# A table of block priorities, new durations in the build-time scheduler, and the first rope on VectorE

## The chip, the core and the metric

The kernel runs on one core of one Trainium2 chip. The engines of the core work side by side, each through its own list of instructions in order: TensorE (PE, matmuls, and PEld, the weight loads beside them), VectorE (DVE), ScalarE (ACT), GpSimd (POOL) and SyncE (SP), which here issues nearly all DMAs. An instruction that needs the work of another engine waits on a semaphore, and everything behind it on its engine waits too. The metric is the time of one execution on the device in microseconds (us), as a median of several runs.

## The reference

Attention over q, k and v with rotary embedding ("rope"), and then a gated MLP over the tokens of all heads together:

```python
batch, n_heads, seq, head_dim = (4, 8, 576, 64)
q_rot, k_rot = (rotate(q), rotate(k))
scores = scale * np.matmul(q_rot, k_rot.transpose(0, 1, 3, 2))
scores = scores - np.max(scores, axis=-1, keepdims=True)
attn = np.exp(scores)
attn = attn / (np.sum(attn, axis=-1, keepdims=True) + 1e-09)
out = np.matmul(attn, v)                       # then (B*S, H*D) = (2304, 512)
...
h = x @ w_in                                   # 512 x 2048
sp = np.where(h > 20.0, h, np.log1p(np.exp(np.minimum(h, 20.0))))
g = h * np.tanh(sp)                            # "mish"
return (g @ w_out).astype(np.float32)          # 2048 x 512
```

## The kernel before

The heads are taken in 16 pairs P (four pairs to a batch), the 576 queries of a pair in five steps t (four of 128 queries for each of the two heads, one of 64). I write (P,t) for a step. A step is: scores on PE into two PSUM pairs (line 569 or 563), the row maximum on DVE (577), exp on ACT (579), the reciprocal of the sums on DVE (588, 590). In the first batch (pairs 0 to 3, "exact" steps) PE itself transposes the weights (612, 625, 629), and ACT or DVE copies them to SBUF. In the other batches the weights are split into a high half (POOL 594 or ACT 596) and a low half (DVE 600), and a DMA transpose on SP turns them (678, and 689 for the step of 64). `av(P, k)` multiplies them with v (702 to 715) for the first 256 queries (k = 0, steps 0 and 1) and for the other 320 (k = 1), and ACT (736) and DVE (738) write the result as a high and a low half into `xt`.

Before a step comes the rope of its pair: `rope_turn` loads raw q or k by DMA (459, 462; a ring of three buffers), multiplies by cos and sin (469) and adds (473), in two column halves. All of it ran on POOL. From pair 8 on, ACT and POOL or DVE split the result once more (498 to 520). The weights w_in and w_out arrive as 64-bit numbers and are decoded block by block (829 to 849) on ACT, DVE and POOL during the first batch. v is loaded into a ring of two staging buffers (536, `stg`), scaled on ACT (539, 540), and POOL writes its low half (541) and so frees the buffer.

The MLP goes in eight chunks c (two for a batch, 256 and 320 tokens). `h_unit` does 12 matmuls (935) and mish on ACT (940), `h_split` makes the halves of g (950 or 951, 954), `p_sub` does 12 matmuls on g (971), four of which make an output block that ACT copies (979) and sends out. Exp and mish are in two ACT tables; each change of table is an instruction of its own (ACT_TABLE_LOAD).

All of this is recorded with `op(...)` as a list of operations with their possible engines, a duration in ns for each, and what they read and write. `Plan.order` then plays the list through at build time: it keeps a clock for each engine, and whenever one is free it gives it the ready operation with the lowest `prio` (the place in the list plus a shift, less a share of the longest chain behind it). What comes out is the order of the instructions of each engine, SP's DMAs among them. Where the plan has PE idle ahead of a matmul that takes a new PSUM buffer, `fill` puts matmuls on the identity there (1072), whose result nobody uses, to keep TensorE's clock up.

Of the kernel before, what the change touches and what calls it, by code (L numbers as in the profile page):

```python
# [39 lines left out]
TR = 107 / 128  # L40
ALPHA = 7
SLOTS = [
# [20 lines left out]
SWITCH = 1400  # L63
DWELL = 0
PEN = 202
PENP = 1
HOLD = 0
PE, ACT, DVE, POOL, SP = "PE", "ACT", "DVE", "POOL", "SP"


# [14 lines left out]
class Plan:  # L85
# [4 lines left out]
    def __init__(self):  # L90
        self.ops, self.rings, self.shift, self.banks = [], {}, 0, []

    def tile(self, pool, shape, dt, tag, bufs=1):
# [13 lines left out]
    def op(self, ways, w=(), r=(), table=None, after=()):  # L107
# [5 lines left out]
        o = {"ways": ways, "deps": set(), "users": [], "n": len(self.ops), "bufs": []}  # L113
        o["prio"] = o["n"] + self.shift
        if table:
# [25 lines left out]
    def order(self):  # L141
# [25 lines left out]
        ready_at = [0.0] * len(ops)  # L167
        free = dict.fromkeys((PE, ACT, DVE, POOL, SP), 0.0)
        ring_free = dma_free = 0.0
# [31 lines left out]
        while len(issued) < len(ops):  # L201
# [5 lines left out]
            for e in (PE, ACT, POOL, DVE, SP):  # L207
# [3 lines left out]
                while ready[e] or other:  # L211
# [58 lines left out]
                    else:  # L270
# [8 lines left out]
                        if e == PE:  # L279
                            if ops[n]["takes"] and 8000 < now < WARM:  # L280
                                b = ops[n]["takes"][0]
                                ends = [until(x) for x in held]
                                one = sum(ends[i] <= now for i in kinds[1])
                                at = min(ends[i] for i in kinds[2 if b.size == 2 or one <= b.keep else 1])
                                idle = 0.8 * (now - max(free[PE], at))
                                if idle > 350:
                                    while now - idle >= window + 3413:
                                        warm = busy > 2900 or (warm and busy > 1540)
                                        busy, window = max(busy - 3413, 0), window + 3413
                                    m = ops[n]["fill"] = int(idle / (108 if warm else 215))  # L290
                                    busy += m * (108 if warm else 215)
# [56 lines left out]
def pool_ns(n):  # L348
    return 2.39 * n + 20
# [15 lines left out]
def attention_mish_mlp(ctx: ExitStack, tc: tile.TileContext, qk, v, vflat, rope, ident_in, w_in, w_out, outT):  # L365
# [56 lines left out]
    def max_exponent(am, cols, lo, hi, out=None):  # L422
# [4 lines left out]
        pt = bank()  # L427
        op((PE, 110, lambda: nc.tensor.transpose(pt()[0:1, 0:128], m(), ident())), w=[pt], r=[m, ident])
        t = small((1, 1))
# [3 lines left out]
        pb = bank()  # L433
        op((PE, 60, lambda: nc.tensor.matmul(
            pb()[:, 0:1], e().to_broadcast([1, 128]), ident()[0:1, 0:1], start=True, stop=True)), w=[pb], r=[e, ident])
# [18 lines left out]
    def rope_turn(P, j, out=None, late=0):  # L454
# [9 lines left out]
        for c, s in enumerate(halves):  # L464
# [13 lines left out]
            op([(POOL, pool_ns(m), lambda f=add: f(nc.gpsimd), 1), (DVE, dve_ns(m), lambda f=add: f(nc.vector), 1)][:n],  # L478
               w=[(t, c) if out is None else (out, (j, c))], r=[(t, c), (t, 2 + c)])
# [104 lines left out]
    def inverse(sm, n, scale=2.0 ** -15):  # L584
        r = sbuf((128, 2), F32, "rs", 3)
        for h in range(n):
            c = slice(h, h + 1)
            op((DVE, 70, lambda c=c: nc.vector.tensor_scalar(sm()[:, c], sm()[:, c], 1e-9, scale, op0=ALU.add, op1=ALU.mult)),  # L588
               w=[(sm, h)])
            op((DVE, 80, lambda c=c: nc.vector.reciprocal(r()[:, c], sm()[:, c])), w=[(r, h)], r=[(sm, h)])  # L590
        return r
# [392 lines left out]
    def mlp(c):  # L984
        for u in range(8):
            for _ in h_unit(c, u):
                yield "h"
            if u >= 1:
                h_split(c, u - 1)
        h_split(c, 7)  # L990
        for e in range(4):
            for s in range(4):
                p_sub(c, e, s)
                yield "p"
# [15 lines left out]
    END = len(seq) + AVL + 1  # L1010

    def att(i):
        for f, a in aux.pop(i, []):
            f(*a)
        if i < len(seq):
            step(*seq[i])
        for f, a in aux.pop(("av", i), []):
            f(*a)

# [117 lines left out]
```

## Time and profile before

| what | value |
|---|---|
| time, median of 3 runs | 648.72 us (647.25 to 649.4) |
| profiled execution, span from the first to the last instruction | 652.7 us |
| PE busy | 615.1 us, 94% |
| ACT, DVE, POOL busy | 466.5, 414.9 and 270.9 us |
| mean granted TensorE clock | 0.991 |
| DMAs of SP | 60 transposes, 30 loads of raw q and k, 12 of v, and others |

The page gives the profiled execution's span alone as its own time; it lies 4.0 us over the median of the runs without a profile. A PE that is busy is not a PE that does needed work: the identity matmuls of `fill` count as busy. Idle time of an engine is put down to the instruction that ended it.

### The profile page before, as it was taken

The numbers are of one execution on the slowest core, as the hardware profiler recorded it, in microseconds if no ns is written. First come the engines' busy times: TensorE is split into PE (matmuls) and PEld (weight loads), VectorE is DVE, ScalarE is ACT, GpSimd is POOL, SyncE is SP. The second block draws the span as 40 slices with busy tenths as digits, with TensorE's granted clock in tenths as the row PEclk, the third lists the DMA queues.
The fourth block names the chain that finished last, engine by engine and source line by source line (L and its number), as shares of the span: only waits on it lengthen the run. The fifth ranks groups of instructions, "written<-read, shape, count | busy, mean of one in ns | idle before, by whom it ended". The sixth has DMA issues, their size and how long they took to land.

```text
span 652.7 us, 13278 instructions
## 1 busy us (share of the span) xinstructions
PE 615.1 (94%) x5218; PEld 458.3 (70%) x5218; DVE 414.9 (64%) x955; ACT 466.5 (71%) x856; POOL 270.9 (42%) x267
## 2 busy tenths in 40 slices
PE   3988889999998999899999999899999999999997
PEld 2665566777775656578877776588877777888775
DVE  0799999787586877747567777576567876211210
ACT  1679979999678995569979885597769956522520
POOL 5489878776937143433454355242212110000000
PEclk9998999999999999999999999899999999999999
DMA  8975415355396668755557664834344578000000
GB/s 321 422 277 173 165 65 170 105 186 159 122 199 123 146 127 189 128 118 93 118 119 160 110 156 100 167 62 74 71 89 91 76 146 137 13 9 17 9 12 31
DMA packets 143583, 82.52 MB, mean 126 GB/s; under 512 B 128160, under 2 KB 133920, under 8 KB 141984
## 3 DMA queue, kind: packets, MB, share of 16 engines
q1 hardware_dynamic: 138912, 76.95, 48.9%
q10 hardware_dynamic: 4608, 4.72, 2.2%
q8 instruction: 41, 0.67, 0.4%
q14 instruction: 22, 0.18, 0.1%
HBM read 45.09 MB, written 4.72 MB: 76 GB/s over the span
## 4 chain that ended last, share of the span: by engine, by line
PE 54%; DMA 2%; POOL 1%; issue 1%; ACT 1%; DVE 1%; DVEq 0%; POOLq 0%; ACTq 0%
PE bank L971 21%; PE bank L935 21%; PE pair L569 5%; PE bank L714 4%; DMA et<-ew 2%; PE pair L935 1%; PE pair L563 1%; PE bank L710 1%; DMA stg<-in_v 1%; POOL v L541 0%; POOL raw L473 0%; ACT e L579 0%; DVE mx L577 0%; POOL ew L594 0%; PE bank L715 0%
## 5 line engine op out<-in xcount | busy, mean ns | idle before, releaser
L971 PE MATMUL bank<-g,w 128*128 128x256 f16 (+1 forms) x1536 | 200.2, 287 | 0.9 <-DVE g L954 0.9
L935 PE MATMUL bank<-xt,w 128*128 128x320 f16 (+1 forms) x1440 | 187.0, 286 | 0.0
L971 PEld LDWEIGHTS <-w 128*128 128x128 f16 x1536 | 147.1, 98 | 47.6 <-issue 11.0
L935 PEld LDWEIGHTS <-w 128*128 128x128 f16 x1536 | 147.5, 98 | 42.9 <-issue 6.7
L579 ACT ACTIVATE e<-pair,mx 128x576 f32<-128x576 f32 x144 | 105.3, 735 | 37.1 <-DVE mx L577 32.7
L577 DVE TENSOR_REDUCE mx<-pair 128x1 f32<-128x576 f32 x144 | 103.4, 750 | 42.1 <-PE pair L569 38.2
L594 POOL TENSOR_SCALAR ew<-e,rs 128x576 f16<-128x576 f32 x68 | 51.3, 760 | 184.6 <-ACT e L579 94.4
L469 POOL TENSOR_TENSOR raw<-raw,cs 128x576 f32<-128x576 f32 (+2 forms) x64 | 90.1, 1425 | 42.7 <-DMA raw<-in_qk 42.2
L600 DVE SCALAR_TENSOR_TENSOR ew<-e,rs,ew 128x576 f16<-128x576 f32 x108 | 98.6, 949 | 13.3 <-ACT ew L596 7.3
L954 DVE SCALAR_TENSOR_TENSOR g<-mh,cells,g 128x512 f16<-128x512 f32 (+1 forms) x64 | 54.8, 865 | 65.5 <-ACT g L950 65.3
L569 PE MATMUL pair<-qk 64*128 64x288 f32 (+1 forms) x704 | 85.5, 362 | 3.5 <-ACT e L579 3.4
L940 ACT ACTIVATE mh<-bank,cells 128x256 f32<-128x256 f32 (+1 forms) x120 | 56.9, 500 | 43.9 <-PE bank L935 40.9
L569 PEld LDWEIGHTS pair<-qk 64*128 64x128 f32 (+1 forms) x704 | 54.7, 180 | 25.3 <-issue 11.4
L588 DVE TENSOR_SCALAR sm<-sm 128x1 f32<-128x1 f32 x144 | 21.4, 151 | 50.3 <-ACT e L579 49.5
L579 ACT ACT_TABLE_LOAD x37 | 47.5, 1283 | 3.6 <-DVE mx L577 2.8
L940 ACT ACT_TABLE_LOAD x38 | 48.8, 1283 | 1.4 <-ACT ot L979 0.8
L950 ACT ACTIVATE g<-mh,cells 128x512 f16<-128x512 f32 (+1 forms) x57 | 43.5, 774 | 1.3 <-PE bank L971 0.4
L979 ACT ACTIVATE ot<-bank,cells 128x256 f32<-128x256 f32 (+1 forms) x32 | 15.8, 495 | 38.9 <-PE bank L971 38.8
L715 PE MATMUL bank<-et,v 128*64 128x256 f16 (+1 forms) x288 | 41.8, 297 | 0.0
L714 PE MATMUL bank<-et,v 128*64 128x256 f16 (+1 forms) x288 | 41.8, 297 | 0.0
L1072 PEld LDWEIGHTS <-ident 128*128 128x128 f16 x246 | 24.9, 104 | 22.0 <-DMA ident<-in_ident 11.1
L596 ACT ACTIVATE ew<-e,rs 128x576 f16<-128x576 f32 x40 | 30.3, 772 | 11.1 <-ACT e L579 6.6
(129 smaller groups left out, 746.8 us busy)
## 6 DMA issues: line engine op xcount, KB each, us to landing
raw<-in_qk SPq DMA_DIRECT2D x30, 576.0 KB, 4.2
w<-in_w_in SPq DMA_DIRECT2D x4, 1024.0 KB, 10.5
stg<-in_v SPq DMA_DIRECT2D x12, 320.0 KB, 3.1
stg<-in_vflat SPq DMA_DIRECT2D x9, 384.0 KB, 3.3
w<-in_w_out SPq DMA_DIRECT2D x3, 1024.0 KB, 4.9
out_dram<-ot ACTq DMA_DIRECT2D x16, 160.0 KB, 2.1
g<-in_w_in SPq DMA_DIRECT2D x2, 1024.0 KB, 16.0
xt<-in_w_out SPq DMA_DIRECT2D x2, 1024.0 KB, 5.2
```

Source lines behind the costliest of these rows:

```text
L469: e.tensor_tensor(out=t()[:, :, s], in0=t()[:, :, s], in1=cs()[:, :, s], op=ALU.mult)
L569: nc.tensor.matmul(out, x[own, q], y[own, s], **kw)
L577: op((DVE, dve_ns(S), lambda: nc.vector.tensor_reduce(m(), pt()[:, :, :HS], axis=AX.XY, op=ALU.max, negate=True)), w=[m], r=[pt])
L579: op((ACT, act_ns(S, psum=True, ptr=2), lambda: nc.scalar.activation(e().rearrange("p (c s) -> p c s", c=2), pt()[:, :, :HS], AF.Exp, bias ...
L594: op([(POOL, 1.27 * S, lambda: nc.gpsimd.tensor_scalar(w()[:, c], e(), r()[:, h:h + 1], 1.0, op0=ALU.mult, op1=ALU.mult), 1), (ACT, act_ns ...
L600: op((DVE, dve_ns(S) + 61, lambda: nc.vector.scalar_tensor_tensor(out=w()[:, c], in0=e(), scalar=r()[:, h:h + 1], in1=w()[:, hc], op0=ALU. ...
L714: nc.tensor.matmul(po()[0:64, :n], V()[:, vi, c, 0:64], et[:, c, :], start=False, stop=last)
L935: nc.tensor.matmul(hp(), w1()[:, wi, cc, f:f + 128], x()[:, xi, cc, q0:q0 + n], start=cc == 0 and a == 0, stop=cc == NCC - 1 and a == 2)
L940: op((ACT, act_ns(n, psum=True, ptr=1), lambda j=j, hp=hp: nc.scalar.activation(hn()[:, j, :n], hp(), AF.Mish, scale=uh())), w=[(hn, j)], ...
L950: op([(ACT, act_ns(2 * n, ptr=1), lambda: nc.scalar.activation(g()[:, 0, f, :n], hn()[:, :, :n], AF.Copy, scale=f32(gs))), (DVE, dve2_ns(2 ...
L954: op((DVE, dve_ns(2 * n) + 61, lambda: nc.vector.scalar_tensor_tensor(out=g()[:, 1, f, :n], in0=hn()[:, :, :n], scalar=f32(gs), in1=g()[:, ...
L971: nc.tensor.matmul(pp()[:, :n], w2e[e]()[:, wi, f], g()[:, gi, f % 8, :n], start=f == 0 and a == 0, stop=f == NF - 1 and a == 2)
```

## The change

Three things. First, the planner: `ORDER` holds a number for each block (a block is a step, a load, an `h_unit`, a `p_sub` and so on, marked with `plan.mark`), and the operations of a block get that number in place of their place in the list; the constants ALPHA, DWELL, PEN and PENP, some durations and the conditions for fill matmuls are new too. Second, the DMA of the identity is recorded ahead of the rope table, and has a number of its own. Third, for pair 0 the first choice of engine for the rope is VectorE instead of GpSimd. The work itself, the tiles and their buffers stay.

```diff
-ALPHA = 7
+ALPHA = 7.992
...
-DWELL = 0
-PEN = 202
-PENP = 1
+DWELL = 920.788
+PEN = 800
+PENP = 183.99
...
+ROPED = (0,)
+ORDER = {}
+for _row in """
+    load_ident: =-891.8
+    load_cs: 0=-4725.3 1=-2736.9
...
+    def mark(self, *name):
+        self.name = name = "_".join(str(x) for x in name)
+        self.blk = self.names.setdefault(name, len(self.names))
...
-        o["prio"] = o["n"] + self.shift
+        o["prio"], o["blk"] = o["n"] + self.shift, self.blk
+        name = self.name
+        if name in ORDER:
+            o["prio"] += ORDER[name] - self.base.setdefault(name, o["prio"])
...
-        free = dict.fromkeys((PE, ACT, DVE, POOL, SP), 0.0)
+        free = dict.fromkeys((PE, ACT, DVE, POOL, SP), 700.0)
...
-                            if ops[n]["takes"] and 8000 < now < WARM:
+                            if ops[n]["takes"] and now < WARM:
...
-                                idle = 0.8 * (now - max(free[PE], at))
+                                idle = 0.8 * (now - max(free[PE], at, 4500.0))
...
-        op((PE, 110, lambda: nc.tensor.transpose(pt()[0:1, 0:128], m(), ident())), w=[pt], r=[m, ident])
+        op((PE, 250, lambda: nc.tensor.transpose(pt()[0:1, 0:128], m(), ident())), w=[pt], r=[m, ident])
...
-            n = 2 if P < NP else 1
-            op([(POOL, pool_ns(2 * m), lambda f=mul: f(nc.gpsimd), 1), (DVE, dve_ns(2 * m), lambda f=mul: f(nc.vector), 1)][:n],
+            n, w = 2 if P < NP else 1, -1 if P in ROPED else 1
+            op([(POOL, pool_ns(2 * m), lambda f=mul: f(nc.gpsimd), 1), (DVE, dve_ns(2 * m), lambda f=mul: f(nc.vector), 1)][:n][::w],
...
-        op((DVE, dve_ns(S) + 61, lambda: nc.vector.scalar_tensor_tensor(
+        op((DVE, dve_ns(S) + 180, lambda: nc.vector.scalar_tensor_tensor(
...
+        plan.mark("load_ident")
+        op((SP, dma_ns(128 * 128 * 4), lambda: nc.sync.dma_start(ident(), ident_in)), w=[ident])
         for c, s in enumerate((slice(0, CUT), slice(CUT, S))):
+            plan.mark("load_cs", c)
             op((SP, dma_ns(256 * (s.stop - s.start) * 4), lambda s=s: nc.sync.dma_start(cs()[:, :, s], rope[:, :, s])), w=[(cs, c)])
-        op((SP, dma_ns(128 * 128 * 4), lambda: nc.sync.dma_start(ident(), ident_in)), w=[ident])
```

The order that the planner makes can be read from the built programs. Three places follow; the line numbers of the changed kernel are higher by 79 to 95.

SP at the start of the program, first before and then now (cs is the rope table, raw the q and k of the pairs, w and xt are homes of w_in):

```order
L1052 DMA cs<-in_rope 128x2x320
L1052 DMA cs<-in_rope 128x2x256
L459 DMA raw<-in_qk 128x2x320 x2
L459 DMA raw<-in_qk 128x2x256 x2
L462 DMA raw<-in_qk 128x1152
L1053 DMA ident<-in_ident 128x128
L778 DMA w_68<-in_w_in 128x1024 x4
```

```order
L1147 DMA cs<-in_rope 128x2x320
L1147 DMA cs<-in_rope 128x2x256
L538 DMA raw<-in_qk 128x2x320
L538 DMA raw<-in_qk 128x2x256
L1144 DMA ident<-in_ident 128x128
L538 DMA raw<-in_qk 128x2x320
L538 DMA raw<-in_qk 128x2x256
L541 DMA raw<-in_qk 128x1152
L857 DMA w_68<-in_w_in 128x1024 x2
```

The identity moved from the eighth place of the queue to the fifth, not to the first; the two halves of k of pair 0 stand ahead of it and those of q behind.

DVE at the start, before and now (mx is the row maximum of the first scores, cells<-w a maximum over w_in):

```order
L791 TENSOR_REDUCE cells<-w_68 128x1
L577 TENSOR_REDUCE mx<-pair_77 128x1
L577 TENSOR_REDUCE mx<-pair_78 128x1
L588 TENSOR_SCALAR sm<-sm 128x1
L791 TENSOR_REDUCE cells<-w_68 128x1
```

```order
L548 TENSOR_TENSOR raw<-raw,cs 128x2x320
L548 TENSOR_TENSOR raw<-raw,cs 128x2x256
L552 TENSOR_TENSOR qk<-raw 128x320
L552 TENSOR_TENSOR qk<-raw 128x256
L548 TENSOR_TENSOR raw<-raw,cs 128x2x320
L548 TENSOR_TENSOR raw<-raw,cs 128x2x256
L552 TENSOR_TENSOR qk<-raw 128x320
L552 TENSOR_TENSOR qk<-raw 128x256
L656 TENSOR_REDUCE mx<-pair_77 128x1
L656 TENSOR_REDUCE mx<-pair_78 128x1
L870 TENSOR_REDUCE cells<-w_68 128x1
```

All eight operations of the first rope, k and then q, now stand at the head of DVE's list, and the first maximum over w_in behind the first two maxima of scores.

SP in the third batch (pairs 8 to 11), in before from the transposes of steps (10,0) to (10,2), and now from the two loads ahead of that of (8,4) (stg<-in_v is the load of v, raw<-in_qk of later pairs' q and k, et the turned weights):

```order
L678 DMA_TRANSPOSE et<-ew 128x18x128 x3
L462 DMA raw<-in_qk 128x1152
L678 DMA_TRANSPOSE et<-ew 128x18x128
L462 DMA raw<-in_qk 128x1152
L536 DMA stg<-in_v 128x640 x2
L678 DMA_TRANSPOSE et<-ew 128x18x128 x2
L689 DMA_TRANSPOSE et<-ew 128x18x64
```

```order
L541 DMA raw<-in_qk 128x1152 x2
L768 DMA_TRANSPOSE et<-ew 128x18x64
L757 DMA_TRANSPOSE et<-ew 128x18x128 x4
L541 DMA raw<-in_qk 128x1152
L615 DMA stg<-in_v 128x640
L541 DMA raw<-in_qk 128x1152
L757 DMA_TRANSPOSE et<-ew 128x18x128
L768 DMA_TRANSPOSE et<-ew 128x18x64
L757 DMA_TRANSPOSE et<-ew 128x18x128
L615 DMA stg<-in_v 128x640
L757 DMA_TRANSPOSE et<-ew 128x18x128 x2
```

In before the last two loads of v stand one behind the other, ahead of the transposes of steps (11,0), (11,1) and (10,4). Now they stand apart, six and three transposes earlier, and two loads of raw q and k stand together ahead of the transposes of steps (8,4) and (8,3).

## Rows read from the trace of the kernel before

**Rows 1.** Windows by stage: length, busy PE, PEld, DVE, ACT, POOL, clock, DMA, GB/s.

```profile
0.00:18.50 18.50, 7.39 (x44) 5.41 (x44) 1.22 (x1) 2.88 (x4) 11.89 (x16) 1.00 0.89 334
...
18.50:99.10 80.60, 70.24 (x548) 49.49 (x548) 75.72 (x216) 67.70 (x145) 63.80 (x64) 0.98 0.58 215
...
99.10:160.00 60.90, 57.94 (x497) 42.49 (x496) 51.07 (x133) 59.93 (x112) 46.14 (x42) 1.00 0.48 155
...
160.00:280.30 120.30, 115.12 (x921) 77.31 (x920) 86.82 (x202) 89.40 (x167) 58.57 (x56) 0.99 0.71 148
...
404.00:421.50 17.50, 12.90 (x107) 8.73 (x106) 7.77 (x18) 8.83 (x19) 2.93 (x4) 0.90 0.88 154
...
421.50:549.00 127.50, 127.50 (x1174) 99.18 (x1172) 89.79 (x182) 99.69 (x175) 29.21 (x33) 1.00 0.52 96
...
sum 652.70, PE 615.12 PEld 458.30 DVE 414.95 ACT 466.52 POOL 270.88; mean PE 76.89 PEld 57.29 DVE 51.87 ACT 58.31 POOL 33.86
```

**Rows 2.** Windows, identity matmuls (line 1072) alone: length, PE, PEld, clock, DMA, GB/s.

```profile
18.50:99.10 80.60, 24.07 (x191) 18.18 (x190) 0.98 0.58 215
...
sum 652.70, PE 33.47 PEld 24.92; mean PE 8.37 PEld 6.23
```

**Rows 3.** Timeline at the start: start us, length us, engine, line, operation.

```profile
4.79 0.67 SPq L1053 DMA_DIRECT2D ident<-in_ident  x1
...
7.37 4.24 POOL L469 TENSOR_TENSOR raw<-raw,cs 128x640 f32<-128x640 f32 x3 [6.08 <-DMA raw<-in_qk]
...
11.11 7.43 PE L1072 MATMUL pair<-ident 128*128 128x256 f16 x42 [11.11 <-DMA ident<-in_ident]
...
11.56 2.36 POOL L473 TENSOR_TENSOR qk<-raw 128x320 f32<-128x320 f32 x3
...
13.27 0.47 ACT L481 ACTIVATE qk<-qk 128x320 f32<-128x320 f32 x1 [11.25 <-POOL qk L473]
...
18.47 1.24 PE L569 MATMUL pair<-qk 64*128 64x288 f32 x8
```

**Rows 4.** Timeline of PE, the first matmuls of the MLP.

```profile
99.08 2.79 PE L935 MATMUL bank<-xt,w 128*128 128x256 f16 x24
```

**Rows 5.** Timeline of PE near 200 us.

```profile
200.17 0.57 PE L710 MATMUL bank<-et,v 128*128 128x320 f16 x3 [1.80 <-DVE sm L588]
```

**Rows 6.** Window with the first dip of the clock after 60 us, PE alone.

```profile
260.00:280.00 20.00, 17.63 (x137) 0.91 0.75 131
```

**Rows 7.** Timeline of ACT, DVE and SP at the first late transposes.

```profile
260.88 0.83 ACT L539 ACTIVATE stg<-stg,cells 128x640 f32<-128x640 f32 x1 [2.73 <-DMA stg<-in_v]
...
263.26 2.29 DVE L600 SCALAR_TENSOR_TENSOR ew<-e,rs,ew 128x576 f16<-128x576 f32 x2
...
265.71 9.78 SPq L678 DMA_TRANSPOSE et<-ew  x3
```

**Rows 8.** Timeline of SP, DVE and POOL near 396 us.

```profile
396.17 5.46 SPq L536 DMA_DIRECT2D stg<-in_v  x2
...
396.39 5.50 DVE L600 SCALAR_TENSOR_TENSOR ew<-e,rs,ew 128x576 f16<-128x576 f32 x4
...
399.36 1.91 POOL L541 TENSOR_TENSOR v<-stg,v 128x640 f16<-128x640 f32 x1
...
401.75 7.46 SPq L678 DMA_TRANSPOSE et<-ew  x2
```

**Rows 9.** Timeline of an undisturbed step, (15,0).

```profile
528.63 1.42 DVE L577 TENSOR_REDUCE mx<-pair 128x1 f32<-128x576 f32 x2
...
531.62 1.55 DVE L600 SCALAR_TENSOR_TENSOR ew<-e,rs,ew 128x576 f16<-128x576 f32 x2 [0.21 <-POOL ew L594]
...
533.31 2.55 SPq L678 DMA_TRANSPOSE et<-ew  x1
```

**Rows 10.** Groups of instructions on ACT: the table loads.

```profile
L940 ACT ACT_TABLE_LOAD x38 | 48.8, 1283 | 1.4 <-ACT ot L979 0.8
...
L579 ACT ACT_TABLE_LOAD x37 | 47.5, 1283 | 3.6 <-DVE mx L577 2.8
```

More of the change, by code (lines that the diff above doesn't have):

```diff
@@ L71 @@
+""".split():
+    if _row.endswith(":"):
+        _kind = _row[:-1]
+    else:
+        _key, _at = _row.split("=")
+        ORDER[f"{_kind}_{_key}" if _key else _kind] = float(_at)
 class Buf:
@@ L91, in __init__ @@
         self.ops, self.rings, self.shift, self.banks = [], {}, 0, []
+        self.blk, self.names, self.base, self.name = 0, {}, {}, ""
+    def mark(self, *name):
+        self.name = name = "_".join(str(x) for x in name)
+        self.blk = self.names.setdefault(name, len(self.names))
     def tile(self, pool, shape, dt, tag, bufs=1):
@@ L433, in max_exponent @@
         pb = bank()
-        op((PE, 60, lambda: nc.tensor.matmul(
+        op((PE, 230, lambda: nc.tensor.matmul(
             pb()[:, 0:1], e().to_broadcast([1, 128]), ident()[0:1, 0:1], start=True, stop=True)), w=[pb], r=[e, ident])
@@ L473, in add @@
                 e.tensor_tensor(out=to, in0=t()[:, 0, s], in1=t()[:, 1, s], op=ALU.add)
-            n = 2 if P < NP else 1
-            op([(POOL, pool_ns(2 * m), lambda f=mul: f(nc.gpsimd), 1), (DVE, dve_ns(2 * m), lambda f=mul: f(nc.vector), 1)][:n],
+            n, w = 2 if P < NP else 1, -1 if P in ROPED else 1
+            op([(POOL, pool_ns(2 * m), lambda f=mul: f(nc.gpsimd), 1), (DVE, dve_ns(2 * m), lambda f=mul: f(nc.vector), 1)][:n][::w],
                w=[(t, c), (t, 2 + c)], r=[(cs, c)] if P < PLAIN else [(cs, 0), (cs, 1)])
-            op([(POOL, pool_ns(m), lambda f=add: f(nc.gpsimd), 1), (DVE, dve_ns(m), lambda f=add: f(nc.vector), 1)][:n],
+            op([(POOL, pool_ns(m), lambda f=add: f(nc.gpsimd), 1), (DVE, dve_ns(m), lambda f=add: f(nc.vector), 1)][:n][::w],
                w=[(t, c) if out is None else (out, (j, c))], r=[(t, c), (t, 2 + c)])
@@ L587, in inverse @@
             c = slice(h, h + 1)
-            op((DVE, 70, lambda c=c: nc.vector.tensor_scalar(sm()[:, c], sm()[:, c], 1e-9, scale, op0=ALU.add, op1=ALU.mult)),
+            op((DVE, 125, lambda c=c: nc.vector.tensor_scalar(sm()[:, c], sm()[:, c], 1e-9, scale, op0=ALU.add, op1=ALU.mult)),
                w=[(sm, h)])
-            op((DVE, 80, lambda c=c: nc.vector.reciprocal(r()[:, c], sm()[:, c])), w=[(r, h)], r=[(sm, h)])
+            op((DVE, 135, lambda c=c: nc.vector.reciprocal(r()[:, c], sm()[:, c])), w=[(r, h)], r=[(sm, h)])
         return r
@@ L985, in mlp @@
         for u in range(8):
+            plan.mark("h", c, u)
             for _ in h_unit(c, u):
                 yield "h"
+                plan.mark("h", c, u)
             if u >= 1:
+                plan.mark("split", c, u - 1)
                 h_split(c, u - 1)
+        plan.mark("split", c, 7)
         h_split(c, 7)
@@ L992, in mlp @@
             for s in range(4):
+                plan.mark("p", c, e, s)
                 p_sub(c, e, s)
@@ L1010, in attention_mish_mlp, with mark @@
     END = len(seq) + AVL + 1
+    def mark(f, a):
+        if f is shifted:
+            f, a = a[1], a[2:]
+        plan.mark(f.__name__, *a)
     def att(i):
         for f, a in aux.pop(i, []):
+            mark(f, a)
             f(*a)
         if i < len(seq):
+            plan.mark("step", *seq[i])
             step(*seq[i])
         for f, a in aux.pop(("av", i), []):
+            mark(f, a)
             f(*a)
```

60 lines of the change are left out of this document (added).

## The prediction

> **What bounds the kernel now.** I read the busy times by stage first. PE is busy for 615.1 of 652.7 us, so 37.6 us are idle; but 33.5 us of the busy time are identity matmuls, which only fill holes [rows 1, 2]. Together 71 us in which PE does nothing needed. The stages show where. Up to 18.5 us PE has no work at all (11.1 us idle, the rest identity matmuls). From 18.5 to 99.1 it is idle for 10.4 us and fills for 24.1 us, while DVE is busy for 75.7 of 80.6 us, ACT for 67.7 and POOL for 63.8: here the first batch's attention and the decoding of the weights bound the kernel, and PE waits for them. At 99.1 us the MLP's first matmuls come [rows 4], and from there PE has two sources of work: 3.0 us idle up to 160 us, 5.2 us from 160 to 280, 4.6 us from 404 to 421.5, and none from 421.5 to 549 (1174 matmuls in 127.5 us). The reader is to see in these rows that a faster engine pays only before about 100 us, and after that only where PE stops at a named wait.
>
> There are three such waits. At 200.17 us an `av` waits 1.8 us [rows 5]. Between 260 and 280 us PE is idle for 2.4 us and the granted clock is 0.91, so some 18% of the 20 us ran at 1.2 instead of 2.4 GHz, which costs half of 3.6 us, 1.8 us [rows 6]. Its cause: ACT stood still for 2.7 us at a scaling of v whose DMA had not landed, ahead of the exp of step (7,1); the low halves of (7,0) stood on DVE behind that exp's sums and came only at 263.26; three transposes then went out one after another, 9.78 us in all, and the `av` of pair 7, on which the next chunk waits, needed the second of them [rows 7]. The third is the dearest: 4.6 us idle from 404 to 421.5 and a clock of 0.90, which costs half of 20% of 17.5 us, 1.75 us; 6.35 us together [rows 1]. There SP held two loads of v for 5.46 us, the second until POOL had freed a staging buffer at 401.27, and the transposes of (11,0), (11,1) and (10,4) stood behind them in SP's queue although (10,4) and (11,0) were finished on DVE at about that time or before [rows 8].
>
> **The change, part by part.** *The start.* Eight operations of the first rope leave POOL, where four multiplications at 1.41 and four additions at 0.79 us cost 8.8 us (4.24/3 and 2.36/3), and go to DVE, which did nothing until 13 us [rows 1, 3]. The trace has no such operation on DVE; the nearest row with two SBUF inputs is 1.55/2 = 0.775 us for 576 columns [rows 9], 1.35 ns a column. I take that: 0.86, 0.69, 0.43 and 0.35 us for 640, 512, 320 and 256 columns, 2.3 us for k and as much for q. The first half of k lands at 7.37 us, as POOL's first multiplication shows, and its DMA keeps its place. k is done at 9.7. q's DMAs stand behind the identity now, which takes SP 0.67 us, so its halves land about 9.5 us: 0.86 + 0.69 + 0.43 us after 9.7 its first half is done (11.7), ACT scales it in 0.47 us, and the first scores could start at about 12.3. But 19 identity matmuls stand ahead of them on PE. The identity landed 6.3 us after its issue at 4.79; issued at about 3.2 it lands at 9.5, and 19 times 7.43/42 = 0.177 us end at 12.9. I take 13.5 for the first scores, with the cold first ones, against 18.47 now: **-5.0 us**. It is worth that only if what follows moves with it; since DVE, ACT and POOL are 94, 84 and 79% busy from there to 99.1 with work whose total the change leaves as it is, I let it. Bounds: 0, if the weights' DMAs (busy share 0.89 and more at first) set the pace instead, and -9, if POOL's 8.8 us and the new order also pack DVE and ACT tighter.
>
> *The wait at 200 us.* Ahead of the `av` of (4, k=1) PE's list had about 11.7 us of matmuls behind its last scores, and now has 20 (counted in the order, twelve matmuls of 128x320 at 1.63 us): **-1.8**.
>
> *The wait at 270 us.* Now the scaling of v stands one step earlier on ACT, ahead of step (7,0), and its DMA ahead of the transpose of (6,2), so ACT has no reason to stop. But PE's list holds only 13.3 us between the scores of (7,1) and its `av` (12.7 before), and DVE still does the low halves of (7,1) behind the maxima of (7,2). An undisturbed step takes from its maximum at 528.63 to the end of its transpose at 535.86 7.2 us, and most late ones 8 to 10 [rows 9]; with maxima 4.4 us later in between I get 12 to 15. Of 4.2 us I let half go: **-2.0**, bounds 0 and -4.2.
>
> *The wait at 410 us.* The two loads of v stand apart now, six and three transposes earlier, each behind a point where POOL has freed its buffer by its own order. **-6.0** of 6.35, bound -2.
>
> *New narrow places.* Between the scores and the `av` of (10, k=0), (13, k=0) and (14, k=1) PE's list holds 12.4, 11.1 and 8.5 us, where before it held 28.5, 20 and 14.4. Against 8 to 10 us for a chain, and 2 for its landing, I add **+2.0**, bounds 0 and +7.
>
> *At nothing:* 75 table loads become 57, 18 times 1.283 = 23.1 us of ACT [rows 10]; ACT is busy for at most 84% where PE waits on it and less later, so the gain is hidden behind PE's matmuls; it would count only where ACT ends a wait. 41 more identity matmuls stand in holes. The new durations matter through the order alone.
>
> Sum: -5.0 - 1.8 - 2.0 - 6.0 + 2.0 = -12.8, so 639.9 us for a span of 652.7. That span is 4.0 us over the median of the runs; on their scale 635.9, say **636 us**.
>
> **Rivals.** *The start gains nothing.* The MLP's first matmuls wait for the last high and low half of the first four `av`. In DVE's list 213 instructions stood ahead of the fourth low half; now 265, by their mean durations 24 us more, of which 4.6 are the rope at an idle time. So the MLP starts near 112 us instead of 99, while PE has done three more steps. If PE stays idle or fills for 43% of those 13 us, as it did from 18.5 to 99.1 ((10.4 + 24.1)/80.6), 5.6 us go again: 641. For it: DVE has no slack. Against it: the steps done early are work that PE had to do later.
>
> A neighbour of this comes from a lock. Where POOL's operations stand beside DVE's with two SBUF inputs, DVE's are longer: four low halves took 5.50 us, 1.38 each, against 0.775 in the quiet step [rows 8, 9]. If each of two or three rope operations waits for one POOL multiplication of 1.41, the scores come 2.8 to 4.2 us later, and the start is worth -1 to -2 us: 639 to 640. The Trainium skill (SBUF — State Buffer, section "SBUF: two separate sides") says that such a pair of ports is held for a whole instruction and the other engine fully blocks; the trace agrees as far as 1.38 against 0.775 goes. By the rule alone all eight would wait, 11.3 us, and the start would lose; I do not follow it so far, since POOL's first input lands at about 10.5, when five are done.
>
> *Packed tighter.* If DVE and ACT go to 97% in the first 160 us, the start gives -9 and the narrow places nothing: 630.
>
> *Slower: SP's queue again.* A load that waits for its buffer holds every transpose behind it, and one such place cost 6.35 us. The new order has three: two loads of raw ahead of (8,4) and (8,3), raw, v, raw ahead of (9,3), and two raw ahead of (10,3). If all three hold as the old one did, 636 + 19 = 655; from two on it is level with before. For it: the second load at the first place needs POOL to finish a k of pair 11 (line 518), which stands behind step (8,4)'s high half; I count some 14 us from the scores of (8,3) to there, and the `av` comes at 23. Against it: at the other two the buffer is free by POOL's order.
>
> *The change does not do what it says.* The identity is not loaded first but fifth, as the order shows; that alone is 1.6 us of the start and in the sum already. If the whole table only exchanged one set of holes for another: 648.
>
> **Chances.** The forecast, 631 to 640: 0.50. The start gains nothing, or the lock: 0.20. Packed tighter: 0.13. Slower by the queue: 0.09. Level: 0.08, half of it within 0.3% (which is about what this measurement can tell from no change). The range, 626 to 648, reaches below to most of the tight case (all bounds for the better together, 652.7 - 9 - 1.8 - 4.2 - 6.35 - 4.0, give 627) and above to the narrow places at their bound beside a start of 0 (648). Faster 0.85, same 0.05, slower 0.10.
>
> **What would show it.** Right: the first scores at 13 to 14 us with DVE busy from 7.4; the first MLP matmul later than 99 us, near 110; step (4,0)'s scores at 153 to 157 instead of 160; no PE wait of over 2 us at an `av` between 160 and 550; 57 table loads. Wrong: SP transposes that go out more than 5 us after their last low half near (8,3), a new dip of the granted clock after 160 us, or PE idle and fill times before 100 us as large as now. The prediction fails if the engines of the first 100 us do not keep their pace, since that is where the kernel loses most.

## The result and the profile after

The changed kernel takes 644.07 us (median of 20 runs, 642.1 to 649.5), the kernel before beside it 648.89 us (20 runs, 646.75 to 654.8): ratio 0.9914, interval [0.9891, 0.9937], so 4.8 us faster by the medians and 5.6 by the ratio. The forecast was 636, 12.8 us faster. The time lies in the range of 626 to 648, but less than half of the forecast gain came.

The profiled execution of the changed kernel spans 640.8 us, and the forecast sum had 639.9. So the sum agrees with the traces (652.7 to 640.8 is -11.9) and not with the timed runs. Both facts have to be explained, and the first turns out to be luck.

The busy times by stage of the changed kernel (start:end, length, PE, PEld, DVE, ACT, POOL, clock, DMA share, GB/s; in the rows for 255:290 and 400:430 PE alone; stages overlap):

```profile
0.00:18.50 18.50, 10.03 (x65) 6.63 (x66) 8.81 (x17) 5.23 (x10) 6.56 (x12) 1.00 0.85 324
18.50:99.10 80.60, 71.83 (x565) 49.80 (x563) 75.35 (x212) 70.35 (x150) 64.66 (x61) 0.98 0.61 229
99.10:114.80 15.70, 14.21 (x123) 10.37 (x124) 14.15 (x40) 13.19 (x32) 14.38 (x15) 1.00 0.44 167
0.00:160.00 160.00, 140.58 (x1128) 100.02 (x1128) 131.77 (x360) 130.71 (x267) 117.88 (x114) 0.99 0.57 208
255.00:290.00 35.00, 34.34 (x310) 1.00 0.69 141
290.00:400.00 110.00, 108.57 (x975) 83.46 (x971) 72.19 (x144) 82.26 (x149) 47.85 (x45) 1.00 0.57 124
400.00:430.00 30.00, 28.89 (x280) 1.00 0.58 119
426.00:548.00 122.00, 121.74 (x1113) 94.03 (x1111) 79.48 (x166) 88.29 (x160) 22.50 (x28) 1.00 0.52 92
```

And its identity matmuls alone (line 1166) in the same view:

```profile
0.00:18.50 18.50, 5.88 (x33) 3.96 (x34) 1.00 0.85 324
18.50:99.10 80.60, 27.10 (x210) 19.58 (x210) 0.98 0.61 229
99.10:114.80 15.70, 5.75 (x45) 4.22 (x45) 1.00 0.44 167
0.00:160.00 160.00, 38.72 (x287) 27.76 (x287) 0.99 0.57 208
```

The same view of the kernel before: a stretch in whole and in its identity matmuls alone, then three windows behind 160 us (PE alone in the first and last):

```profile
99.10:114.80 15.70, 14.40 (x123) 10.24 (x123) 14.09 (x37) 15.64 (x34) 14.39 (x14) 1.00 0.50 162
99.10:114.80 15.70, 1.53 (x11) 1.07 (x11) 1.00 0.50 162
...
255.00:290.00 35.00, 32.63 (x270) 0.95 0.78 157
290.00:400.00 110.00, 110.00 (x1007) 85.70 (x1006) 78.58 (x172) 94.95 (x164) 54.09 (x55) 1.00 0.55 117
400.00:430.00 30.00, 25.40 (x219) 0.94 0.72 141
```

I call busy PE less identity matmuls the needed work; it is a time, so a matmul that ran at the lower clock counts for more. By 160 us it is 140.58 - 38.72 = 101.9 us. Before it was 7.39 + 70.24 + 57.94 - 33.47 = 102.1 us [rows 1, 2], all identity matmuls lying ahead of 160 us. In all, the first 160 us gained nothing. They gained at first: by 99.1 us the changed kernel has 10.03 + 71.83 - 5.88 - 27.10 = 48.9 us of needed work and the kernel before 46.2 [rows 1, 2], whose identity matmuls ahead of 18.5 us take 7.39. From 99.1 to 114.8 us, while the kernel before has the MLP to work on and the changed kernel does not yet, it is 14.21 - 5.75 = 8.5 against 14.40 - 1.53 = 12.9, so 4.4 us are lost again; 1.5 come back by 160 us. A second trace of the changed kernel (eighth run below) has 48.6 and 8.5 in the same two stretches and 101.5 by 160 us.

What was gained in the traces lies behind 160 us: the two stages that held the waits at 270 and 410 us now run at clock 1.00, and 400 to 430 is idle for 1.1 us, where before it lost 4.6 us idle and 1.8 to the clock. Against that PE is idle for 1.4 us from 290 to 400, where it was idle for none, and for 0.3 from 426 to 548, where it was idle for none either [rows 1].

The start, in the timeline of the changed kernel (start us, length us, engine, line, operation):

```profile
7.35 1.43 DVE L548 TENSOR_TENSOR raw<-raw,cs 128x640 f32<-128x640 f32 x2 [7.35 <-DMA raw<-in_qk]
8.21 4.24 PE L1166 MATMUL pair<-ident 128*128 128x256 f16 x19 [8.21 <-DMA ident<-in_ident]
8.69 0.82 DVE L552 TENSOR_TENSOR qk<-raw 128x320 f32<-128x320 f32 x2
9.43 1.42 DVE L548 TENSOR_TENSOR raw<-raw,cs 128x640 f32<-128x640 f32 x2
10.77 0.82 DVE L552 TENSOR_TENSOR qk<-raw 128x320 f32<-128x320 f32 x2
11.31 2.90 POOL L548 TENSOR_TENSOR raw<-raw,cs 128x640 f32<-128x640 f32 x2 [10.02 <-DMA raw<-in_qk]
12.38 1.29 PE L648 MATMUL pair<-qk 64*128 64x288 f32 x8
...
114.77 1.47 PE L1014 MATMUL bank<-xt,w 128*128 128x256 f16 x12
```

The first scores come at 12.38 instead of 18.47 us [rows 3], the MLP's first matmuls at 114.77 instead of 99.08 [rows 4].

What PE waited for behind 160 us, in the view of waits (engine, line, releaser, us in total, times, longest), and SP's queue in the third batch, in the timeline:

```profile
PE bank L789 <- DMA et<-ew: 2.2, 3, 1.3
PE pair L1014 <- ACT e L658: 1.3, 1, 1.3
PE bank L1014 <- ACT mh L1019: 0.3, 1, 0.3
```

```profile
304.92 10.63 SPq L541 DMA_DIRECT2D raw<-in_qk  x2
316.39 2.12 SPq L768 DMA_TRANSPOSE et<-ew  x1
...
377.03 5.37 SPq L541 DMA_DIRECT2D raw<-in_qk  x2
390.44 5.61 SPq L757 DMA_TRANSPOSE et<-ew  x2
```

No load of v stands right ahead of the transposes at 390.44 any more, as two did for 5.46 us [rows 8], and no `av` (line 789) waits over 1.3 us. Two pairs of loads of q and k still hold SP, for 10.63 and 5.37 us.

### The profile page after: what moved, and what is told of

Its sections match the earlier page's. It is cut to its first block, busy times and chain, and to the rows that moved or that the text cites. A ratio compares the mean times of both kernels' runs of the same rounds, so it can differ in the third digit from the quotient of the medians.

```text
span 640.8 us, 13358 instructions
## 1 busy us (share of the span) xinstructions
PE 614.2 (96%) x5259; PEld 458.7 (72%) x5259; DVE 417.7 (65%) x958; ACT 449.4 (70%) x851; POOL 258.4 (40%) x251
## 5 line engine op out<-in xcount | busy, mean ns | idle before, releaser
L1050 PE MATMUL bank<-g,w 128*128 128x256 f16 (+1 forms) x1536 | 197.7, 286 | 0.0
L1014 PE MATMUL bank<-xt,w 128*128 128x256 f16 (+1 forms) x1332 | 171.6, 286 | 0.4 <-ACT mh L1019 0.3
L673 POOL TENSOR_SCALAR ew<-e,rs 128x576 f16<-128x576 f32 x62 | 47.3, 767 | 185.7 <-DVE rs L669 99.9
L679 DVE SCALAR_TENSOR_TENSOR ew<-e,rs,ew 128x576 f16<-128x576 f32 x108 | 99.1, 941 | 16.0 <-POOL ew L673 9.2
L548 POOL TENSOR_TENSOR raw<-raw,cs 128x576 f32<-128x576 f32 (+2 forms) x60 | 86.4, 1461 | 41.6 <-DMA raw<-in_qk 41.4
L1019 ACT ACTIVATE mh<-bank,cells 128x320 f32<-128x320 f32 (+1 forms) x111 | 52.3, 499 | 35.4 <-PE bank L1014 34.1
L675 ACT ACTIVATE ew<-e,rs 128x576 f16<-128x576 f32 x46 | 35.0, 771 | 13.2 <-ACT e L658 5.6
L1029 ACT ACTIVATE g<-mh,cells 128x640 f16<-128x640 f32 (+1 forms) x53 | 41.1, 777 | 2.5 <-PE bank L1050 1.5
L1166 PEld LDWEIGHTS <-ident 128*128 128x128 f16 x287 | 27.8, 101 | 17.3 <-DMA ident<-in_ident 8.2
L793 PE MATMUL bank<-et,v 128*64 128x256 f16 (+1 forms) x288 | 39.8, 288 | 0.0
L794 PE MATMUL bank<-et,v 128*64 128x256 f16 (+1 forms) x288 | 39.8, 288 | 0.0
```

The source lines that it names most:

```text
L548: e.tensor_tensor(out=t()[:, :, s], in0=t()[:, :, s], in1=cs()[:, :, s], op=ALU.mult)
L673: op([(POOL, 1.27 * S, lambda: nc.gpsimd.tensor_scalar(w()[:, c], e(), r()[:, h:h + 1], 1.0, op0=ALU.mult, op1=ALU.mult), 1), (ACT, act_ns ...
L679: op((DVE, dve_ns(S) + 180, lambda: nc.vector.scalar_tensor_tensor(out=w()[:, c], in0=e(), scalar=r()[:, h:h + 1], in1=w()[:, hc], op0=ALU ...
L793: nc.tensor.matmul(po()[0:64, :n], V()[:, vi, c, 0:64], et[:, c, :], start=False, stop=last)
L1014: nc.tensor.matmul(hp(), w1()[:, wi, cc, f:f + 128], x()[:, xi, cc, q0:q0 + n], start=cc == 0 and a == 0, stop=cc == NCC - 1 and a == 2)
L1019: op((ACT, act_ns(n, psum=True, ptr=1), lambda j=j, hp=hp: nc.scalar.activation(hn()[:, j, :n], hp(), AF.Mish, scale=uh())), w=[(hn, j)], ...
```

## The experiments

Ratios are to runs of the kernel before on the same chip, with a 95% interval. Up to the twelfth run the intervals reach 1.5 to 2 us either way.

**First, second, ninth and tenth run: the kernel before, traced again.** No edit.

> The kernel before, unchanged, timed against itself and traced a second time. In the traces the change took 11.9 us (652.7 to 640.8), in the medians 4.8 us. Theory 'long execution': the trace on which the forecast stood was a long execution, and one or more of the three late waits (1.8 us at 200, 4.2 to 5.3 at 270, 6.35 at 404 to 421) is much smaller in most executions; a second trace then spans 644 to 649 us and shows at least one of them below half of its size. Rival 'fixed waits': the waits come from the order and stand in every execution; a second trace then shows 4 us or more of idle PE and slow clock between 404 and 422 and at least 4 around 270, whatever its span. Ratio 1.000 within 0.003 by both.

> The kernel before, a third trace. As for the second one: by 'long execution' a span of 644 to 649 us and late waits of other sizes than in the first trace; by 'fixed waits' the same 10 us or so of lost PE time between 200 and 422.

> The kernel before, a fourth trace. Theory 'the waits vary': the late waits (PE idle and slow clock) at 200, 270 and 404 to 421 us change in size between executions of one order; over the traces so far that hold them they came to 1.9 to 4.9, 2.5 to 4.9 and 4.3 to 7.6 us, and the first trace stood near the upper end with 14.9 us in all. A fresh trace has a sum of 9 to 14 us and a span of 646 to 653 that goes with it. Rival 'tracing lengthens this kernel': again 651 to 655 with 13 to 15 us in the three waits, as in the three traces before, while timed runs have a median span of 648.

> The kernel before, a fifth trace. As for the fourth: 'the waits vary' 646 to 653, and its span stands over the fourth's by about as much as its three waits do; 'tracing lengthens this kernel' 651 to 655 again.

Against itself it measured 649.0 us, ratio 0.9998 [0.997, 1.0026]. The four traces span 651.2, 654.6, 649.9 and 648.0 us. Two windows of each, PE alone (the waits at 270 and at 410 us); the second trace:

```profile
255.00:290.00 35.00, 32.90 (x288) 1.00 0.83 167
400.00:430.00 30.00, 26.38 (x227) 0.94 0.87 140
```

the third:

```profile
255.00:290.00 35.00, 32.53 (x265) 0.95 0.87 164
400.00:430.00 30.00, 28.28 (x242) 0.94 0.73 141
```

the fourth:

```profile
255.00:290.00 35.00, 32.68 (x271) 0.95 0.85 166
400.00:430.00 30.00, 28.33 (x258) 1.00 0.75 142
```

the fifth:

```profile
255.00:290.00 35.00, 32.89 (x291) 1.00 0.81 163
400.00:430.00 30.00, 27.44 (x252) 1.00 0.73 142
```

The reader is to add the idle time of a window (length less PE) and what the clock took (length times 1 less the clock). At 410 us that gives 5.4, 3.5, 1.7 and 2.6 us, against 6.35 in the first trace [rows 1]: on average 3.9. At 270 us it gives 2.1, 4.2, 4.1 and 2.1, against 4.1. SP's hold itself is much the same (5.0 to 5.5 us in all five): the two loads took 5.46 us in the first trace [rows 8] and in the fifth

```profile
395.14 5.45 SPq L536 DMA_DIRECT2D stg<-in_v  x2
400.72 6.92 SPq L678 DMA_TRANSPOSE et<-ew  x2
```

but what PE loses by it changes, in part by whether the clock falls (it does in the first three traces at 410 us and not in the last two). The waits stand in each trace, as "fixed waits" had it, but not with their size. "The waits vary" is right on that. "Long execution" had expected spans of 644 to 649 us; the second and third trace are longer, so it is not borne out in that form. "Tracing lengthens this kernel" is not borne out either: the fourth and fifth trace span 0.5 us more and 1.4 less than the median span (649.4) of the 16 runs on the same chip. But the second and third span 2.7 and 6.1 us more than the median (648.5) of the 41 runs on theirs, so a part of it stays open.

**Third run: one load of v later.** In the kernel before, a dependency that only the planner sees:

```diff
-        load("v", dma_ns(128 * 640 * 4), lambda dma: dma(tv(), v[P]), w=[t])
+        load("v", dma_ns(128 * 640 * 4), lambda dma: dma(tv(), v[P]), w=[t]); P == 15 and plan.ops[-1]["deps"].add(st["turn", 11, 1])
...
-            op((SP, turn_ns(128 * 4 * S * 2), lambda: nc.sync.dma_start_transpose(
+            st["turn", P, t] = op((SP, turn_ns(128 * 4 * S * 2), lambda: nc.sync.dma_start_transpose(
```

> The kernel before with one DMA moved: the load of v of pair 15 goes out on SP three transposes later, behind those of (11,0), (11,1) and (10,4), and not ahead of them; PE's list is the same to the last matmul. By the forecast's price of the wait at 410 us, 5 to 6.35 us less: 642.5 to 644, ratio 0.990 to 0.992, which would be all that the change won. By 'long execution' the wait is smaller in most runs: 0 to 3 us less, ratio 0.995 to 1.000.

647.25 us, ratio 0.9948 [0.9925, 0.9971]: 3.4 us, between 1.9 and 4.9. Its window and SP's queue:

```profile
400.00:430.00 30.00, 30.00 (x287) 1.00 0.70 139
```

```profile
395.72 0.33 SPq L536 DMA_DIRECT2D stg<-in_v  x1
398.36 6.38 SPq L678 DMA_TRANSPOSE et<-ew  x2
406.66 1.12 SPq L536 DMA_DIRECT2D stg<-in_v  x1
```

The transposes go out 3.4 us earlier than in the first trace (398.36 against 401.75) and PE is not idle in the whole window. One moved DMA, with PE's list the same, so the cause of that wait is shown. Its price in timed runs is near the mean of the five traces, 3.9, and not what the first had.

**Fourth run: the changed kernel, its first rope back on GpSimd.** The lambdas that VectorE had for pair 0 call GpSimd (the part of the line that changes):

```diff
-(DVE, dve_ns(2 * m), lambda f=mul: f(nc.vector), 1)
+(DVE, dve_ns(2 * m), lambda f=mul: f(nc.vector if P else nc.gpsimd), 1)
```

and the same for the addition. The order stays the one that was made for the rope on VectorE.

> The changed kernel with the eight operations of the first rope put back on GpSimd at the same places of the order; all else stays. The first scores should come 3 to 6 us later, at 15.5 to 18.5 us. If the start's gain is kept to the end (forecast: 5.0 us), the time is 3 to 5 us over the changed kernel, 647 to 649, ratio to before 0.997 to 1.000. If it is lost again before the first MLP matmuls ('the start gains nothing'), the time stays within 1.5 us of the changed kernel: 643 to 645.5, ratio 0.990 to 0.995.

648.51 us, ratio 0.9969 [0.9945, 0.9993]. The changed kernel had 0.9914 and, in the eighth run, 0.9927, so the rope on VectorE is worth 0.4 to 0.55% in this order, 2.7 to 3.6 us, close to the 3 to 5 that were expected if the start's gain is kept to the end. In the trace it is more:

```profile
7.77 2.75 POOL L548 TENSOR_TENSOR raw<-raw,cs 128x640 f32<-128x640 f32 x2 [6.47 <-DMA raw<-in_qk]
16.10 2.29 PE L648 MATMUL pair<-qk 64*128 64x288 f32 x8 [3.90 <-ACT qk L560]
```

```profile
12.00:30.00 18.00, 13.47 (x94) 9.77 (x93) 9.59 (x26) 9.26 (x21) 12.46 (x15) 0.81 1.01 424
0.00:160.00 160.00, 136.87 (x1075) 97.55 (x1075) 122.03 (x335) 124.76 (x256) 120.83 (x116) 0.96 0.56 202
```

```profile
0.00:160.00 160.00, 39.94 (x287) 28.28 (x287) 0.96 0.56 202
```

The scores come 3.7 us later; PE stood still for 3.9 us ahead of them, its first eight matmuls took 2.29 us instead of 1.29, and from 12 to 30 us the granted clock was 0.81. Needed work by 160 us is 136.87 - 39.94 = 96.9, 4.9 less than in the changed kernel, and 5.2 less than before; the five traces of the kernel before have 100.0 to 103.2, so one trace gives such a difference to about 1.5 us. So the rope on VectorE does bring something that is kept. Without it this order would be behind by 160 us; how far behind an order made for the rope on GpSimd would be, no run shows. What the change brings without it is 0.31%, 2.0 us, by the timed runs.

**Fifth run: the start alone, in the old order.** The mirror of the edit above in the kernel before, and `fill` cut to 8 matmuls in its first call instead of 42.

> The kernel before with the start alone changed: the eight operations of the first rope on VectorE at their old places of the order, and 8 identity matmuls ahead of the first scores in place of 42; all later work in the old order. First scores at 12.5 to 14 us instead of 18.5. If the start's gain is kept to the end, as the forecast of -5.0 us has it, and as the rope was worth 4 us in the changed kernel's order: 644 to 646 us, ratio 0.991 to 0.994. If the engines of the first 100 us swallow it: 648 to 650, ratio 0.998 to 1.001, with the first MLP matmuls still near 98 to 99 us.

646.22 us, ratio 0.9957 [0.9932, 0.9983]: 2.8 us, which lies between the two ratios that were expected (a start kept to the end, a start swallowed). The interval goes from 1.1 to 4.4 us.

**Sixth run: the scaling of v of pair 10 later on ScalarE.** A planner dependency of that instruction on the exps of (7,1).

> The kernel before with one ScalarE instruction moved: the scaling of v of pair 10 stands behind the two exps and the first high half of step (7,1), not ahead of them. In the trace ACT no longer stops 2.7 us at that place and the av of (7, k=0) no longer waits 2.4 us at 275. If that wait is worth in the timed runs what it is in the trace (4.2 to 5.3 us with what stands behind it), ratio 0.992 to 0.994; by the forecast, which let half of 4.2 go, 0.996 to 0.998; if the chain of (7,1) is as late without it, 1.000.

650.46 us, ratio 1.001 [0.9983, 1.0036]. The stop of 2.7 us is gone and the window at 270 us reads

```profile
255.00:290.00 35.00, 33.84 (x296) 1.00 0.72 150
```

so 1.2 us lost in place of 2.1 to 4.2, and yet the timed runs gained nothing clear of noise: the interval allows a gain of 1.1 us. In this trace the window at 410 us lost 6.0 us (PE 25.80 of 30 us, clock 0.94), so a part may have gone over to the next wait; the two runs with both edits below have no wait at 410 us to take it. The first trace's chain of causes at 270 us was right as a sequence, and its price in time is too small to be told from nothing.

**Seventh, eleventh and twelfth run: these edits together, in the old order.** All three; the load and the scaling; the start and the load.

> The kernel before with three small edits together: the start of the fifth run, the load of v of pair 15 three transposes later as in the third, the scaling of v of pair 10 behind the exps of (7,1) as in the sixth. No table, no new durations. If the prices add: -4 for the start, -2.5 to -3.4 for the load, -1 to -3 for the scaling, 638.5 to 642 us, ratio 0.984 to 0.989, faster than the changed kernel. If the table is worth more than these three places: 643 or more, ratio 0.991 or above.

> The kernel before with the two late edits together and the old start: the load of v of pair 15 later (third run) and the scaling of v of pair 10 behind the exps of (7,1) (sixth run). Against the three edits together, 641.0, it shows what the start is worth: 2.8 to 4 us, so 643.5 to 645.5, ratio 0.991 to 0.994. If it is as fast as the three edits, the start is worth nothing beside them; if it is no faster than the load alone (647.3), the scaling is worth nothing.

> The kernel before with the start of the fifth run and the load of v later, without the scaling. If the scaling is worth nothing, as the sixth run alone had it: 641 to 642 us, as the three edits. If it is worth 1 to 2 us once the later wait is gone: 642.5 to 643.5, ratio 0.989 to 0.992.

641.01 us, ratio 0.9875 [0.985, 0.9901]; 645.92, 0.9927 [0.9904, 0.9949]; 641.41, 0.9871 [0.9842, 0.99]. The seventh came out as expected if the prices add, the twelfth as expected if the scaling is worth nothing. The start and one load, a handful of lines without a table, beat the changed kernel (0.9914 and 0.9927). The seventh run is the best comparison, since the eighth timed the changed kernel on the same chip: 641.01 against 644.48. The pairs give a price for each edit more than once. Start: 2.8 us alone, 0.9871/0.9948 = 5.0 us beside the load, 0.9875/0.9927 = 3.4 beside both. Load: 3.4 alone, 0.9871/0.9957 = 5.6 beside the start, 0.9927/1.001 = 5.4 beside the scaling. Scaling: nothing alone, 0.9927/0.9948 = 1.4 beside the load, nothing beside both (0.9875 against 0.9871). Such a quotient of two ratios is known to some 2 us either way (an estimate from their intervals), so the prices of one edit do not differ clearly. In the twelfth run:

```profile
7.66 2.31 DVE L469 TENSOR_TENSOR raw<-raw,cs 128x640 f32<-128x640 f32 x3 [7.66 <-DMA raw<-in_qk]
11.53 1.89 PE L1072 MATMUL pair<-ident 128*128 128x256 f16 x8 [11.53 <-DMA ident<-in_ident]
13.34 2.29 PE L569 MATMUL pair<-qk 64*128 64x288 f32 x8
...
96.10 1.16 PE L935 MATMUL bank<-xt,w 128*128 128x256 f16 x9
```

```profile
0.00:160.00 160.00, 133.34 (x1075) 95.09 (x1076) 134.78 (x365) 133.62 (x266) 115.36 (x114) 1.00 0.59 208
```

```profile
0.00:160.00 160.00, 28.54 (x212) 20.88 (x212) 1.00 0.59 208
```

First scores 5.1 us earlier, the MLP 3.0 us earlier (96.10 against 99.08), needed work by 160 us 133.34 - 28.54 = 104.8. The fifth and seventh run, with the same start, have 103.3 and 106.3; the eight traces of the old order with the old start (five of the kernel before, and the third, sixth and eleventh run) 100.0 to 103.2, a mean of 102.0. The first eight matmuls of the scores take 2.29 us here as in the fourth run, behind eight identity matmuls that take 0.24 us each, so that length alone is no sign of the stop ahead of them. Of 5 us at the first scores 3 are left where the MLP begins, and 2.8 by 160 us.

**Eighth run: the changed kernel again.**

> The changed kernel once more, on the chip of the three others, with a second trace. Time 642 to 645, ratio 0.989 to 0.994. Theory 'the excess of before's traces is the wait at 410': the three traces of before span 651.2 to 654.6 while its timed runs have a median span of 648; the changed kernel has no such wait, so its trace spans 640 to 644, as its timed runs do. Rival 'every first, traced execution is some 4 us longer': 644 to 648.

644.48 us, ratio 0.9927 [0.99, 0.9955], span of the trace 641.7. Both traces of the changed kernel span less than the median span of its timed runs (642.3 and 642.7), so the rival, that a traced execution is always some 4 us longer, is out.

**Thirteenth to fifteenth run: parts of the table.** The changed kernel with an empty `ORDER`; without the numbers of the first batch's blocks; with these alone (written short: `first` stands for a test of the block's name, and holds for the loads of identity and rope table, the weights' loads and decoding, pairs 0 to 3, and the first two chunks of the MLP):

```diff
+ORDER = {}
...
+ORDER = {k: v for k, v in ORDER.items() if not first(k)}
...
+ORDER = {k: v for k, v in ORDER.items() if first(k)}
```

> The changed kernel with an empty table: new constants and durations, identity recorded ahead of the rope table, first rope on VectorE, every block at its place in the list. VectorE's list holds 187 instructions ahead of the low half that releases the MLP, against 243 in the changed kernel, so the MLP should start near 95 us instead of 115. If the table's first part is what takes the start's gain back: needed PE work by 160 us 103 us or more. If the constants and durations do: 102 or less, as in the changed kernel. The time depends on the late waits, which nothing removes here: 643 to 652.

> The changed kernel with the table's numbers for the loads, the decoding, pairs 0 to 3 and the first two chunks of the MLP left out, the rest kept. The releasing low half stands at 197, so the MLP starts near 97 us. If the first part of the table takes the start's gain back and its later part removes the waits: needed work by 160 us 103 or more, and 638 to 643 us, ratio 0.983 to 0.990, faster than the changed kernel. If the first part is harmless: 644 or more, ratio 0.992 and up.

> The changed kernel with the table's numbers kept only for the blocks that the fourteenth leaves out. The releasing low half stands at 175 here, since the later blocks no longer push in ahead of it, so the MLP starts near 95 to 100 us. If it is the order of the first blocks itself that costs: needed work by 160 us 102 or less. If it is their mixing with later ones that delays the MLP: 103 or more. Time 643 to 652, since the late waits are the old list's.

681.67, 669.15 and 693.7 us; ratios 1.0471 [1.0419, 1.0524], 1.0295 [1.0254, 1.0335] and 1.0684 [1.0641, 1.0728]. No theory expected that. With the new constants, durations and start but no table the kernel is 4.7% slower than before, with half a table 3 to 7%. In the thirteenth run PE waits for 11.4 us for exps behind 160 us, where it waited 1.5 us for them before and 1.3 in the changed kernel (the view of waits):

```profile
PE pair L650 <- ACT e L660: 11.4, 7, 3.9
```

Its MLP starts at 92.6 us, and its needed work by 160 us is 101.5, no more than in the changed kernel; the fourteenth run has 103.7, the fifteenth 102.2. Five traces of one order spread from 100.0 to 103.2, so these do not differ clearly, and whether the table's first part or the constants take back the start's gain is not settled. The thirteenth run also loses elsewhere: by 114.8 us it has done 63.1 us of needed work, against 57.3 in the changed kernel and 59.0 before, and falls behind only then. So it does not speak against a late MLP as the place of the changed kernel's loss.

## Why the prediction was wrong, point by point

**The scale of the sum failed first.** The step that failed: "That span is 4.0 us over the median of the runs; on their scale 635.9". Each run that lists both has its time 1.7 to 2.0 us over its span (642.61 and 640.8; 653.03 and 651.2). The first trace lists no time; by that it was an execution of some 654.5 us, 5.6 over the median of 648.89, and the 4.0 us were not an offset that the changed kernel has too: its own trace lies 1.5 us under its median. The 8.2 us between 635.9 and 644.07 are 0.9 (639.9 against 640.8), 5.8 (1.8 added where 4.0 was taken off) and 1.5 (642.61 against 644.07).

That the sum met the trace of the changed kernel within 0.9 us was luck. It had -5.0 from the start and -7.8 behind 160 us; the traces have nothing by 160 us, and all of the 11.9 us behind it, 6.0 of them idle PE (13.15 us to 7.14). One term too many and several too small cancelled.

**The wait at 410 us, -6.0.** "-6.0 of 6.35, bound -2" was the right place, the right cause (third run) and the wrong size: five traces have 1.7 to 6.35 with a mean of 3.9, the timed edit 3.4 with the old start and 5.6 with the new. The forecast read the price from the one of five executions that had the most of it. This explains at most 2.5 of the 5.6 us by which the first trace was long; the third trace, the longest, lost only 3.5 at this wait, so the rest stays open.

**The start, -5.0.** "The first scores at 13 to 14 us" was a little too late: they came at 12.38. VectorE's eight operations took 4.5 us, against 4.6 reckoned, and no operation of POOL held them, POOL's first starting at 11.31 when the last addition was under way. So the rival of the lock did not happen, and the rule of the Trainium skill behind it (SBUF — State Buffer, section "SBUF: two separate sides") was not put to the test here: POOL stood idle until then. What failed is "I let it", that what follows moves with the first scores: in the old order the start leaves 2.8 of 5 us by 160 us (104.8 against 102.0), and in the changed kernel nothing is left (101.9 and 101.5). The sum had no term for the reordering of the first batch and the new constants. By the old order with the new start they cost 2.9 us by 160 us, by the fourth run 5.2, which has the order's loss without VectorE's gain.

The rival "the start gains nothing" gave the right outcome: MLP "near 112 us" (114.77), and PE idle or filling for 1.49 + 5.75 = 7.2 of the 15.7 us from 99.1, 46% against the 43% reckoned; before it was 1.3 + 1.5 = 2.8. The place of the loss is thus shown: from 99.1 to 114.8 us both traces of the changed kernel have 8.5 us of needed work, the five of the kernel before 11.6 to 13.0. That the 52 more instructions in DVE's list make it late is only argued, since no run moved the MLP alone.

One sign of the forecast reads its row wrong: the scores at 159.97 us before are matmuls of 64 x 64, a last step of a pair, and not step (4,0), which has 128 queries. They begin at 158.43 now and at 159.67 in the second trace, so 1.5 and 0.3 us earlier where 3 to 7 were expected. And the upper end of the range is added up wrong: a start of 0 and the narrow places at +7 give 635.9 + 5.0 + 5.0 = 645.9, not 648.

**The wait at 200 us, -1.8.** It is gone from both traces of the changed kernel; no edit timed it by itself.

**The wait at 270 us, -2.0.** The window lost 2.1 to 4.2 us in the five traces and loses 0.7 now (the changed kernel has 34.34 us of PE in 255 to 290). But an edit that took 1 to 3 us of it in the trace took nothing from the time that stands clear of noise.

**New narrow places, +2.0.** 1.4 + 1.1 + 0.3 = 2.8 us of idle PE from 290 to 548. Right in size; but the 1.3 us at 342 us are an MLP matmul behind an exp (line 1014), and no `av`.

**At nothing: "The new durations matter through the order alone".** This hid the most: without the table, durations, constants and start together cost 4.7%. The 18 table loads fewer (57 now, as counted) were no gain to be seen.

**SP's queue again, the slower rival.** SP was held, at the first place even for 10.63 us, but what stood behind was not ready: the last copy for the 64 rows that go out at 316.39 ends at 316.37 on DVE, for those at 346.30 at 346.23, and after the hold at 377.03 SP is free for 8 us before the next transpose. PE loses 1.3 us at the most for any one wait. So the holds came and their price did not: in these runs a held queue cost time only where a finished transpose stood in it.

## What to carry to other kernels

Take the price of a wait from several traces, not from one: the same order of instructions lost 1.7 to 6.35 us at one wait, and the trace that a forecast stands on may be the long one; before anything else, put its own time beside the median. A sum that meets the next trace is no proof of its terms; put each stretch beside its own term. To learn what a new order brings, move one instruction at a time in the old one: one load and eight operations of the first rope, moved by hand, with 34 identity matmuls fewer ahead of the first scores, brought 8.4 us, more than the whole change's 4.8 to 5.6. And a table of priorities belongs to the constants that it was made with: with half of it the kernel was slower than without any of the change.

## What the runs showed that was not expected

In one trace a late first operand cost twice: PE that had stood for 3.9 us ahead of the first scores ran at a granted clock of 0.81 from 12 to 30 us, and 3.7 us of delay became 4.9 us of needed work by 160 us. And the program's time goes with the clock that it was granted: of the 41 runs of the kernel before that were timed beside the first four experiments, the 12 with a mean granted clock of 0.997 have a median span of 646.35 us, the 8 with 0.992 one of 650.25. The kernel with three edits, which keeps PE busy from 400 to 430 us, lies between 640.61 and 642.38 in its 6 runs, while the kernel before spreads over 9 us in 26 runs on the same chip; with so few runs the narrower spread is a hint and not shown.
